# Another order of the instructions of the first two heads in a fused attention and soft mixture-of-experts kernel

## The chip, the cores and the metric

The kernel runs on one core of one Trainium2 chip. Times are device microseconds (us) of one execution. A timed run gives one time for the whole program; a profiled execution also gives a trace, whose span runs from the first to the last recorded instruction.

The engines have short names in the rows: PE is TensorE (matrix products), PEld its weight loads, DVE is VectorE, ACT is ScalarE, POOL is GpSimd, and SP the engine that issues nearly all DMA transfers. Each engine takes its own instructions in the order in which they stand in the program, and waits on semaphores for the others.

## The reference

Attention over 8 x 12 heads with 448 rows of 64, causal, and behind it a soft mixture of 8 experts over the 3584 rows of the result:

```
scores = scale * q @ k.T, masked above the diagonal
attn   = exp(scores - max(scores, -1)), divided by its row sum
x      = attn @ v, heads side by side: 3584 x 768
logits = x @ phi                               # 3584 x 32 slots
d      = softmax of logits over the rows       # slot_input = d.T @ x
slot_out[e] = relu(slot_input[e] @ w1[e]) @ w2[e]
out    = softmax of logits over the slots @ slot_out
```

## The kernel before

**Heads and pairs.** The 96 heads are handled one after another by a loop over `i`. Two heads make a pair `p`, whose queries and keys are loaded together; each arrives on 128 partitions as two copies of its 64 rows. In what follows "head 2" is the third head, the first of pair 1.

**What one head needs.** Products are done in a rounded type, with a second product that brings back what rounding lost:

1. `cast_k`, `cast_q` (ACT) round the keys and queries into `ks` and `qd`. `sub_k`, `sub_q` (POOL, or DVE where it says so) subtract the rounded from the raw values: the difference of the keys goes into the lower half of `ks`, that of the queries into `r2` (shown as `r` in rows). `copy_k2` (ACT) copies the rounded keys into `k2` (shown as `k`).
2. `scores1` (PE) multiplies `ks` by `qd` into a PSUM tile `s`, after small products with `tri` that set the causal mask. There are three such tiles, so head i+3 waits until head i has left its tile.
3. `max_evac` (ACT) copies one block row of `s` into `mx`, and `max_keys` 0 to 4 (DVE) take the maximum over the other blocks, transpose in blocks of 32 and reduce, into `r`. `max_row` 0 (PE) transposes that into `rt`, `max_row` 1 (DVE) reduces it into `mr`, and `max_spread` (POOL, an affine select) spreads the negated maximum over 14 rows of `r2`.
4. `scores2` (PE) multiplies `k2` by `r2` onto the same `s`: it adds the correction of the queries and subtracts the maximum. It can't start before `max_spread` of its head.
5. `exps` (ACT) takes the exponential into `pt`, `attv` (PE) multiplies by the values into `po`, and `norm` (DVE) divides.

**The loop.** A table `ORDER` gives the order of these steps in an iteration, one row for the first and one for the second head of a pair. Iteration `i` does the first products of head i+2, the second products and exponential of head i, and `attv` and `norm` of head i-1. So heads 0 and 1, and the first part of head 2, are done before the loop, in an order written out by hand, and the first two iterations leave out steps of the table.

**Warming products.** `warm(n)` issues n products of 128x512 columns that nobody reads; `START` has their numbers at three places of the start.

**Other work of POOL.** The list `later` holds small jobs (memsets and selects for the second half of the kernel); one is taken at the end of an iteration from `i` = 1 on, so they stand between the spreads and differences of the first heads.

**Loads.** SP issues the loads of keys, queries and values in one queue. Those of pair 0 come in halves (one head each), so that work can start early; pair 1's keys and queries are whole loads. The weights of the experts fill 22 resident buffers during attention, and the rest is loaded when buffers of attention come free near its end.

Of the kernel before, what the change touches and what calls it, by code (L numbers as in the profile page):

```python
# [33 lines left out]
RES, TW1 = 22, 12  # L34
WN, PAD = 1536, 24
WARM = (3, 2, 4, 2)
START = (6, 7, 4)

# [40 lines left out]
def attention_soft_moe(ctx: ExitStack, tc: tile.TileContext, qk, va, phi, w1, w2, out):  # L81
    nc = _Core(tc)
# [95 lines left out]
    def warm(n, w=None):  # L178

        w = misc("warm") if w is None else w  # L180
        for _ in range(n):
            nc.tensor.matmul(w, identb, tri.unsqueeze(1).to_broadcast([P, 4, P]),
                             start=True, stop=True)


    def cast_q(p, hs=slice(0, 2)):
        if p < NPAIR:
            nc.scalar.activation(out=qd_[p % NR][:, hs], in_=st["raw", 0, p][:, hs], func=AF.Copy)

    def cast_k(p, hs=slice(0, 2)):  # L190
        if p < NPAIR:
            nc.scalar.activation(out=ks_[p % NR][:, hs], in_=st["raw", 1, p][:, hs], func=AF.Copy)

    def sub_k(p, hs=slice(0, 2), eng=None):
        if p < NPAIR:
            ks = ks_[p % NR][64:P, hs]
            (eng or nc.gpsimd).tensor_tensor(out=ks, in0=st["raw", 1, p][64:P, hs], in1=ks, op=ALU.subtract)

    def copy_k2(p, hs=slice(0, 2)):
        if p < NPAIR:  # L200
            nc.scalar.activation(out=k2_[p % NR][64:P, hs], in_=ks_[p % NR][0:64, hs],
                                 func=AF.Copy)

    def sub_q(p, hs=slice(0, 2), eng=None):
        if p < NPAIR:
            (eng or nc.gpsimd).tensor_tensor(out=r2_[p % NR][64:P, hs], in0=st["raw", 0, p][64:P, hs],
                                             in1=qd_[p % NR][64:P, hs], op=ALU.subtract)
# [29 lines left out]
    def scores1_all(i):  # L237
        for part in ("c0", "k3", "c3", "c12", "k2", "k1", "k0"):
            scores1(i, part)

    def max_evac(i):
        if i < NHD:
            st["mx", i] = (xtp.tile([P, S], F32, tag="xt", name="mx1", bufs=2) if i == 1
                           else mx_)
            nc.scalar.activation(out=st["mx", i], in_=st["s", i][:, SC0:SC0 + S], func=AF.Copy)

    def max_keys(i, k):
        if i >= NHD:
            return
        if k < 3:  # L250
            s, mx = st["s", i], st["mx", i]
            c, w = k + 1, S - CQ0[k + 1]
            nc.vector.tensor_tensor(out=mx[:, CQ0[c]:S], in0=s[:, SCOL[c]:SCOL[c] + w],
                                    in1=mx[:, CQ0[c]:S], op=ALU.max)
        elif k == 3:
            nc.vector.transpose(out=mt_, in_=st.pop(("mx", i)))
        else:
            r = st["r", i] = wk.tile([P, NQB], F32, tag="r", name=f"r{i}", bufs=2)
            nc.vector.tensor_reduce(out=r, in_=mt_.rearrange("p (b k)->p b k", k=32),
                                    axis=AX.X, op=ALU.max)  # L260

    def max_row(i, k):
        if i >= NHD:
            return
        if k == 0:
            st["rt", i] = misc(f"rt{i}")
            nc.tensor.transpose(out=st["rt", i][0:NQB, 0:P], in_=st.pop(("r", i)), identity=ident)
        else:
            mr = st["mr", i] = wk.tile([NQB, 32], F32, tag="mr", name=f"mr{i}", bufs=2)
            nc.vector.tensor_reduce(out=mr, in_=st.pop(("rt", i))[0:NQB, 0:P].rearrange("p (g t)->p t g", g=4),  # L270
                                    axis=AX.X, op=ALU.max, negate=True)

    def max_spread(i):
        if i >= NHD:
            return
        p, h = divmod(i, 2)
        mr = st.pop(("mr", i))

        nc.gpsimd.affine_select(out=r2_[p % NR][0:NQB, h].rearrange("p (b t)->p b t", t=32),
                                in_=mr.unsqueeze(1).to_broadcast([NQB, NQB, 32]),  # L280
                                compare_op=ALU.is_equal, fill=0.0, base=0,
                                pattern=[[-1, NQB], [0, 32]], channel_multiplier=1)

    def scores2(i, cs):
        if i >= NHD:
            return
        p, h = divmod(i, 2)
        s = st["s", i]
        k2, r2 = k2_[p % NR], r2_[p % NR]
        for c in cs:  # L290
            w, m = S - CQ0[c], min(P, S - P * c)
            nc.tensor.matmul(s[0:m, SCOL[c]:SCOL[c] + w], k2[:, h, P * c:P * c + m],
                             r2[:, h, CQ0[c]:S], start=False, stop=True, skip_group_check=True)

    def exps(i):
        if i < NHD:
            nc.scalar.activation(out=pt_[i % 2][:, 0:1024], in_=st.pop(("s", i)), func=AF.Exp, scale=SCALE)
# [149 lines left out]
            plan[o + 19] = lambda b=b: dispatch(b, 1)  # L447


    warm(START[0])  # L450
    h0, h1 = slice(0, 1), slice(1, 2)
    for hs in (h0, h1):
        cast_k(0, hs)
        cast_q(0, hs)
        sub_k(0, hs, nc.vector)
        sub_q(0, hs)
    scores1_all(0)
    scores1_all(1)
    warm(START[1])
    max_evac(0)  # L460
    copy_k2(0, h0)
    max_evac(1)
    cast_k(1, h0)
    cast_k(1, h1)
    cast_q(1, h0)
    copy_k2(0, h1)
    cast_q(1, h1)
    for i, k in ((0, 0), (0, 1), (0, 2), (0, 3), (1, 0), (0, 4), (1, 1), (1, 2)):
        max_keys(i, k)
    sub_k(1, h0)  # L470
    max_row(0, 0)
    scores1_all(2)
    warm(START[2])
    max_evac(2)
    max_row(0, 1)
    max_spread(0)
    max_keys(1, 3)
    max_keys(1, 4)
    sub_k(1, h1, nc.vector)
    sub_q(1, h0)  # L480


    sid = const.tile([P, NSLOT], F32, name="sid")
# [24 lines left out]
    for i in range(NHD + 1):  # L508
        p, h = divmod(i, 2)
        if h:  # L510
            load_qk(p + 3, 1)
            if p + 1 < NPAIR - 1:
                loads_v(p + 1)
            load_qk(p + 3, 0)
            if p % 2 and nload < RES:
                load_w(nload)
                nload += 1
        if i == NHD - 3:

            loads_v(NPAIR - 1, nc.scalar)  # L520
        if i < 2:
            scores2(i, (1, 0, 2))
            if i:
                scores1_all(3)
                max_evac(3)
            scores2(i, (3,))
            exps(i)
            if i == 0:
                max_row(1, 0)
                max_row(1, 1)  # L530
                max_spread(1)
                sub_q(1, h1)

        qs = [int(n[1]) for n in ORDER[h] if n[0] == "a"]
        first = qs[:2] if qs[0] == 3 else qs[:1]
        for n in ORDER[h]:
            if i < 2 and (n in ("ev", "exp") or n[0] in "kt" or n in ("c0", "c3", "c12")):
                continue
            if i == 0 and n in ("mr0", "mr1", "sp"):
                continue  # L540
            if n[0] == "k" or n in ("c0", "c3", "c12"):
                scores1(i + 2, n)
            elif n[0] == "t":
                scores2(i, (int(n[1]),))
            elif n[0] == "a":
                attv(i - 1, (int(n[1]),), first)
            elif n[0] == "x":
                max_keys(i + 2, int(n[1]))
            elif n[0] == "n":
                norm(i - 1, int(n[1]))  # L550
            elif n in ("mr0", "mr1"):
                max_row(i + 1, int(n[2]))
            elif n == "ld":
                if i % 12 == 5 and i > 12:
                    logits_d(i // 12 - 1, lt)
            elif n == "pre":
                pre.get(i, int)()
            elif n == "plan":
                if later and i:
                    later.pop(0)()  # L560
                plan.get(i, int)()
            else:
                {"ev": lambda: max_evac(i + 2), "exp": lambda: exps(i), "sp": lambda: max_spread(i + 1),
                 "ck": lambda: cast_k(p + 2), "sk": lambda: sub_k(p + 2), "cq": lambda: cast_q(p + 2),
                 "c2": lambda: copy_k2(p + 1), "sq": lambda: sub_q(p + 2)}[n]()
        if i == NHD - 1:

            ps = [ps_s.tile([P, 1024], F32, tag="s", name=f"e{k}") for k in range(3)]
            logits_a(NB - 1, (2, 3, 4), ps[0], first=True, last=True)
            logits_t(NB - 1, 1)  # L570

            ph5 = xtp.tile([P, S], F32, tag="xt", name="ph5", bufs=2)[:, 0:P]
            nc.gpsimd.tensor_copy(out=ph5, in_=phis[1][:, 2].unsqueeze(1).to_broadcast([P, 4, NSLOT]))
# [238 lines left out]
```

## Time and profile before

| | us |
|---|---|
| median of 3 runs | 467.39 |
| lowest and highest of these | 465.57, 467.95 |
| the profiled execution's own time | 466.73 |
| its span | 465.0 |

The profiled execution lies between the lowest run and the median; 1.7 us of its time lie outside the span. PE is busy for 93% of the span, DVE for 77%, ACT for 72% and POOL for 59%. These are averages over the attention loop, the change of stages near 375 us, and a last stage in which weights stream in. A change at the start has to be read from the rows of the first 50 us.

### The profile page before, as it was taken

How to read it: one execution, taken by the hardware profiler on the slowest of the kernel's cores; microseconds unless marked ns; L12 is line 12 of the kernel's file. 1: busy time of each engine (PE TensorE's matmuls, PEld its weight loads, DVE VectorE, ACT ScalarE, POOL GpSimd, SP SyncE). 2: the span in 40 equal slices, each digit the busy share in tenths (PEclk: the TensorE clock that was granted, in tenths of full speed). 3: DMA queues.
4: the chain of work that ended last, by engine and by line, in shares of the span. 5: the costliest groups of instructions: out<-in, count | busy, mean ns of one | idle time of the engine just before them, and what ended most of it. 6: DMA issues, size and time to landing. Idle time of an engine off the chain costs nothing.

```text
span 465.0 us, 11809 instructions
## 1 busy us (share of the span) xinstructions
PE 432.1 (93%) x4458; PEld 363.3 (78%) x4458; DVE 356.9 (77%) x1056; ACT 334.2 (72%) x492; POOL 272.4 (59%) x226
## 2 busy tenths in 40 slices
PE   7899999999999999999999999999999999998650
PEld 3798999899899989998999899989989564543220
DVE  5898889888988898899889988988897267523350
ACT  6888898899888979897889789889985211422240
POOL 5898787778777877787777777777873000000000
PEclk9999999999999999999999999999999999999995
DMA  7387767676567666776666776677748989999998
GB/s 257 117 270 232 225 175 234 229 233 215 173 227 245 227 197 189 219 258 211 194 210 214 238 232 187 212 224 233 222 135 307 339 344 418 422 424 421 404 399 327
DMA packets 38200, 119.02 MB, mean 256 GB/s; under 512 B 4096, under 2 KB 11776, under 8 KB 38144
## 3 DMA queue, kind: packets, MB, share of 16 engines
q1 hardware_dynamic: 38000, 118.01, 73.9%
q8 instruction: 35, 0.57, 0.5%
q10 hardware_dynamic: 144, 0.27, 0.2%
q14 instruction: 21, 0.17, 0.1%
HBM read 107.25 MB, written 11.01 MB: 254 GB/s over the span
## 4 chain that ended last, share of the span: by engine, by line
PE 76%; DMA 12%; DVE 2%; ACT 2%; POOL 1%; issue 1%; POOLq 0%; ACTq 0%; SPq 0%
PE po L65 35%; PE s L65 25%; DMA w<-in_w_dram 12%; PE xt L65 5%; PE g L65 2%; PE sp L65 2%; PE rt L65 2%; PE pp L65 1%; PE tp L65 1%; PE hp L65 1%; POOL r L65 1%; PE e L65 1%; ACT ot L65 1%; PE lp L65 1%; POOL ks L65 0%
## 5 line engine op out<-in xcount | busy, mean ns | idle before, releaser
L65 PE MATMUL po<-va,pt 128*128 128x65 f32 (+1 forms) x1920 | 195.9, 250 | 0.1
L65 PEld LDWEIGHTS po<-va,pt 128*128 128x128 f32 (+1 forms) x1920 | 192.6, 171 | 1.3 <-issue 1.0
L65 DVE TENSOR_TENSOR mx<-s,mx 128x320 f32<-128x320 f32 (+2 forms) x288 | 100.6, 349 | 24.6 <-ACT mx L65 21.1
L65 ACT ACTIVATE pt<-s 128x1024 f32<-128x1024 f32 x96 | 98.1, 1021 | 10.9 <-PE s L65 6.7
L65 POOL TENSOR_TENSOR r<-qk,qd 64x896 fp32r<-64x896 f32 (+1 forms) x50 | 101.4, 2029 | 6.8 <-ACT qd L65 2.9
L65 POOL TENSOR_SCALAR_AFFINE_SELECT r<-mr 14x448 fp32r<-14x448 f32 x96 | 61.4, 640 | 73.5 <-DVE mr L65 72.9
L65 POOL TENSOR_TENSOR ks<-qk,ks 64x896 fp32r<-64x896 f32 (+1 forms) x47 | 98.0, 2086 | 5.1 <-ACT ks L65 1.5
L65 PE MATMUL s<-r,k 128*128 128x320 f32 (+3 forms) x384 | 85.0, 300 | 2.6 <-POOL r L65 2.5
L65 PE MATMUL s<-qd,ks 128*128 128x448 f32 (+3 forms) x384 | 77.0, 311 | 1.3 <-DVE ks L65 1.2
L65 ACT ACTIVATE mx<-s 128x448 f32<-128x448 f32 x96 | 52.3, 545 | 30.6 <-PE s L65 29.2
L65 PEld LDWEIGHTS s<-r,k 128*128 128x128 f32 (+1 forms) x384 | 60.0, 176 | 9.1 <-issue 3.7
L65 DVE STREAM_TRANSPOSE mt<-mx 128x448 f32<-128x448 f32 x96 | 61.9, 645 | 3.3
L65 DVE TENSOR_REDUCE r<-mt 128x14 f32<-128x448 f32 x96 | 58.5, 609 | 0.1
L65 PEld LDWEIGHTS s<-qd,ks 128*128 128x128 f32 (+1 forms) x384 | 55.8, 183 | 2.8 <-ACT qd L65 2.0
L65 ACT ACTIVATE ks<-qk 128x896 fp32r<-128x896 f32 (+1 forms) x50 | 45.5, 912 | 3.0 <-DMA qk<-in_qk_dram 3.0
L65 ACT ACTIVATE k<-ks 64x896 fp32r<-64x896 f32 (+1 forms) x49 | 45.8, 934 | 1.2
L65 ACT ACTIVATE qd<-qk 128x896 fp32r<-128x896 f32 (+1 forms) x50 | 46.0, 920 | 0.2
L65 PEld LDWEIGHTS <-identb 128*128 128x128 bf16 x316 | 28.0, 102 | 21.9 <-issue 18.0
L65 DVE TENSOR_TENSOR x<-po,sm 128x256 f32<-128x256 f32 x96 | 40.7, 424 | 3.3
L65 PE MATMUL s<-tri,identb 128*128 128x64 bf16 (+2 forms) x288 | 40.3, 236 | 0.1
L65 ACT ACTIVATE xts<-xt 128x448 f32<-128x448 f32 x47 | 25.4, 541 | 8.2 <-PE xt L65 6.4
L65 PE MATMUL so<-w,ht 128*32 128x384 f32 x256 | 24.7, 492 | 5.9 <-DMA w<-in_w_dram 4.1
(121 smaller groups left out, 417.9 us busy)
## 6 DMA issues: line engine op xcount, KB each, us to landing
w<-in_w_dram SPq DMA_DIRECT2D x64, 768.0 KB, 7.2
qk<-in_qk_dram SPq DMA_DIRECT2D x94, 448.0 KB, 3.4
va<-in_va_dram SPq DMA_DIRECT2D x47, 260.0 KB, 3.5
out_dram<-ot SPq DMA_DIRECT2D x28, 384.0 KB, 7.8
qk<-in_qk_dram SPq DMA_DIRECT2D x4, 224.0 KB, 3.6
va<-in_va_dram ACTq DMA_DIRECT2D x1, 260.0 KB, 3.4
phi<-in_phi_dram SPq DMA_DIRECT2D x2, 48.0 KB, 4.4
```

What stands on the lines that cost most here:

```text
L65: return self._tc.keep_in_program_order(op(*args, **kwargs))
```

## The change

The order of the start is written anew, and two differences of the keys go from DVE to POOL.

- Before the loop, the casts and differences of both heads of pair 0 came first, then the first products of heads 0 and 1, then seven warming products. Now the first head's keys are copied and its scores evacuated before the second head's keys and queries are cast, and four warming products stand between the first products of the two heads. Four further warming products behind the first products of head 2 are gone: 10 in all instead of 17.
- `sub_k` of head 1 and of head 3 run on POOL; before, DVE did them.
- `scores2` and `exps` of head 0 stand ahead of the loop; `sub_q` of heads 1, 2 and 3 come later in POOL's order.
- The first iteration of the loop is written out: `cast_k` and `sub_k` of pair 2, the first products of head 3, part of `attv` of head 0, then `scores2` and `exps` of head 1. The second iteration leaves out what was done there. From iteration 2 on nothing is different.

The core of the diff:

```diff
-START = (6, 7, 4)
+START = (6, 4)
...
-    for hs in (h0, h1):
-        cast_k(0, hs)
-        cast_q(0, hs)
-        sub_k(0, hs, nc.vector)
-        sub_q(0, hs)
+    cast_k(0, h0)
+    cast_q(0, h0)
+    sub_k(0, h0, nc.vector)
+    sub_q(0, h0)
+    copy_k2(0, h0)
     scores1_all(0)
+    max_evac(0)
+    cast_k(0, h1)
+    cast_q(0, h1)
+    sub_k(0, h1)
+    for k in range(5):
+        max_keys(0, k)
+    warm(START[1])
     scores1_all(1)
-    warm(START[1])
-    max_evac(0)
-    copy_k2(0, h0)
+    cast_k(1, h0)
+    copy_k2(0, h1)
+    sub_k(1, h0)
     max_evac(1)
...
+    cast_q(1, h0)
+    for k in range(3):
+        max_keys(1, k)
+    scores1_all(2)
+    cast_k(1, h1)
+    max_evac(2)
+    sub_k(1, h1)
+    scores2(0, (1, 0, 2, 3))
+    sub_q(0, h1)
     max_keys(1, 3)
     max_keys(1, 4)
-    sub_k(1, h1, nc.vector)
-    sub_q(1, h0)
+    exps(0)
+    cast_q(1, h1)
+    max_row(1, 0)
+    max_row(1, 1)
+    max_spread(1)
...
+        if i == 0:
+            for k in range(3):
+                max_keys(2, k)
+            cast_k(2)
+            scores1_all(3)
+            max_evac(3)
+            attv(0, (0, 3), (0,))
+            sub_k(2)
+            max_keys(2, 3)
+            max_keys(2, 4)
+            scores2(1, (1, 0, 2, 3))
+            sub_q(1, h0)
+            copy_k2(1)
+            exps(1)
+            attv(0, (2, 1), ())
+            cast_q(2)
+            continue
...
+            elif n == "sq" and i == 1:
+                sub_q(1, h1)
+                sub_q(2)
```

On POOL the start now reads as follows, up to the spread of head 3. A row has the line, the operation, what it writes and reads, and the shape; `qk_0`, `qk_1`, `qk_2` are the raw keys or queries of pairs 0, 1 and 2, a row that writes `ks` is a `sub_k`, one that writes `r` from `qk` a `sub_q`, and an AFFINE_SELECT is a `max_spread`. Where two rows read alike, the first is the pair's first head, the second its second. Before:

```order
L65 TENSOR_TENSOR r_123<-qk_0_95,qd_118 64x448 x2
L65 TENSOR_TENSOR ks_121<-qk_1_99,ks_121 64x448
L65 AFFINE_SELECT r_123<-mr_210 14x448
L65 TENSOR_TENSOR r_125<-qk_1_101,qd_120 64x448
L65 AFFINE_SELECT r_123<-mr_237 14x448
L65 TENSOR_TENSOR r_125<-qk_1_101,qd_120 64x448
L65 TENSOR_TENSOR ks_119<-qk_2_104,ks_119 64x896
L65 AFFINE_SELECT r_125<-mr_278 14x448
L65 TENSOR_TENSOR r_123<-qk_2_106,qd_118 64x896
L65 MEMSET run_m_226 128x1
L65 AFFINE_SELECT r_125<-mr_324 14x448
```

And of the change, from the second difference on (the first, `sub_q` of head 0, is the same):

```order
L65 TENSOR_TENSOR ks_119<-qk_0_93,ks_119 64x448
L65 TENSOR_TENSOR ks_121<-qk_1_99,ks_121 64x448
L65 AFFINE_SELECT r_123<-mr_186 14x448
L65 TENSOR_TENSOR ks_121<-qk_1_99,ks_121 64x448
L65 TENSOR_TENSOR r_123<-qk_0_95,qd_118 64x448
L65 AFFINE_SELECT r_123<-mr_216 14x448
L65 TENSOR_TENSOR ks_119<-qk_2_104,ks_119 64x896
L65 TENSOR_TENSOR r_125<-qk_1_101,qd_120 64x448
L65 AFFINE_SELECT r_125<-mr_275 14x448
L65 TENSOR_TENSOR r_125<-qk_1_101,qd_120 64x448
L65 TENSOR_TENSOR r_123<-qk_2_106,qd_118 64x896
L65 MEMSET run_m_227 128x1
```

Two differences of 64x448 have come in (the `ks` rows of head 1 and head 3), and of the two `sub_q` of pair 1 both now stand behind the spread of head 1; before, one stood ahead of it.

On ACT, from the first cast to the cast of pair 2's keys; a row `mx` is a `max_evac`, `k` a `copy_k2`, `pt` an `exps`. Before:

```order
L65 ACTIVATE ks_119<-qk_0_93 128x448
L65 ACTIVATE qd_118<-qk_0_95 128x448
L65 ACTIVATE mx<-s_151 128x448
L65 ACTIVATE k_122<-ks_119 64x448
L65 ACTIVATE mx_177<-s_159 128x448
L65 ACTIVATE ks_121<-qk_1_99 128x448 x2
L65 ACTIVATE qd_120<-qk_1_101 128x448
L65 ACTIVATE k_122<-ks_119 64x448
L65 ACTIVATE qd_120<-qk_1_101 128x448
L65 ACTIVATE mx<-s_196 128x448
L65 ACTIVATE pt_85<-s_151 128x1024
L65 ACTIVATE ks_119<-qk_2_104 128x896
```

And of the change, from the two casts of head 1 on:

```order
L65 ACTIVATE ks_119<-qk_0_93 128x448
L65 ACTIVATE qd_118<-qk_0_95 128x448
L65 ACTIVATE ks_121<-qk_1_99 128x448
L65 ACTIVATE k_122<-ks_119 64x448
L65 ACTIVATE mx_182<-s_171 128x448
L65 ACTIVATE qd_120<-qk_1_101 128x448
L65 ACTIVATE ks_121<-qk_1_99 128x448
L65 ACTIVATE mx<-s_193 128x448
L65 ACTIVATE pt_85<-s_148 128x1024
L65 ACTIVATE qd_120<-qk_1_101 128x448
L65 ACTIVATE ks_119<-qk_2_104 128x896
```

The cast of pair 1's first keys now stands ahead of head 1's evacuation, and the second cast of pair 1's queries stands between `exps` of head 0 and the cast of pair 2's keys.

## Rows read from the trace of the kernel before

**Rows 1.** Window: length, busy us (instructions) of five engines, clock, DMA share, GB/s.

```profile
15.20:40.70 25.50, 23.89 (x235) 22.26 (x235) 23.22 (x69) 22.30 (x29) 23.82 (x26) 1.00 0.57 178
```

**Rows 2.** Timeline of POOL, 4 to 46.5 us: start, us, operation [idle before <-releaser].

```profile
10.16 1.13 POOL L65 TENSOR_TENSOR ks<-qk,ks 64x448 fp32r<-64x448 f32 x1 [1.51 <-ACT ks L65]
...
15.21 0.64 POOL L65 TENSOR_SCALAR_AFFINE_SELECT r<-mr 14x448 fp32r<-14x448 f32 x1 [0.87 <-DVE mr L65]
15.93 1.15 POOL L65 TENSOR_TENSOR r<-qk,qd 64x448 fp32r<-64x448 f32 x1
17.03 2.08 POOL L65 TENSOR_TENSOR ks<-qk,ks 64x896 fp32r<-64x896 f32 x1
19.19 0.64 POOL L65 TENSOR_SCALAR_AFFINE_SELECT r<-mr 14x448 fp32r<-14x448 f32 x1
19.91 2.10 POOL L65 TENSOR_TENSOR r<-qk,qd 64x896 fp32r<-64x896 f32 x1
...
22.24 0.64 POOL L65 TENSOR_SCALAR_AFFINE_SELECT r<-mr 14x448 fp32r<-14x448 f32 x1
...
40.07 0.64 POOL L65 TENSOR_SCALAR_AFFINE_SELECT r<-mr 14x448 fp32r<-14x448 f32 x1
...
46.28 0.64 POOL L65 TENSOR_SCALAR_AFFINE_SELECT r<-mr 14x448 fp32r<-14x448 f32 x1 [0.49 <-DVE mr L65]
```

**Rows 3.** Timeline of PE, 1 to 14.5 us and 40 to 42 us.

```profile
7.84 1.20 PE L65 MATMUL s<-qd,ks 128*128 128x192 f32 x3
8.85 2.85 PE L65 MATMUL warm<-tri,identb 128*128 128x512 bf16 x7
...
12.03 0.71 PE L65 MATMUL s<-qd,ks 128*128 128x192 f32 x3
12.58 1.04 PE L65 MATMUL warm<-tri,identb 128*128 128x512 bf16 x4
13.27 0.82 PE L65 MATMUL s<-r,k 128*128 128x320 f32 x4
...
40.77 0.73 PE L65 MATMUL s<-r,k 128*128 128x448 f32 x3 [0.79 <-POOL r L65]
```

**Rows 4.** The tail: timeline of SP, 340 to 400 us.

```profile
346.84 52.97 SPq L65 DMA_DIRECT2D w<-in_w_dram  x30
```

**Rows 5.** Timeline of ACT, 3 to 23 us.

```profile
9.08 0.54 ACT L65 ACTIVATE mx<-s 128x448 f32<-128x448 f32 x1 [0.60 <-PE s L65]
9.52 1.03 ACT L65 ACTIVATE ks<-qk 128x448 fp32r<-128x448 f32 x2
10.55 0.58 ACT L65 ACTIVATE qd<-qk 128x448 fp32r<-128x448 f32 x1
11.15 0.57 ACT L65 ACTIVATE k<-ks 64x448 fp32r<-64x448 f32 x1
...
12.83 0.55 ACT L65 ACTIVATE mx<-s 128x448 f32<-128x448 f32 x1 [0.51 <-ACT qd L65]
14.13 1.02 ACT L65 ACTIVATE pt<-s 128x1024 f32<-128x1024 f32 x1 [0.75 <-PE s L65]
15.05 0.94 ACT L65 ACTIVATE ks<-qk 128x896 fp32r<-128x896 f32 x1
```

**Rows 6.** DMA issued from 2.5 to 3 us: size, us from issue to landing.

```profile
qk<-in_qk_dram SPq DMA_DIRECT2D x1, 448.0 KB, 6.8
```

**Rows 7.** Timeline of DVE, 3.8 to 17.8 us.

```profile
6.84 0.62 DVE L65 TENSOR_TENSOR ks<-qk,ks 64x448 fp32r<-64x448 f32 x1 [2.17 <-ACT ks L65]
...
13.58 1.25 DVE L65 TENSOR_TENSOR ks<-qk,ks 64x448 fp32r<-64x448 f32 x1
14.86 0.28 DVE L65 TENSOR_REDUCE mr<-rt 14x32 f32<-14x128 f32 x1
15.17 1.14 DVE L65 TENSOR_TENSOR mx<-s,mx 128x192 f32<-128x192 f32 x3
...
17.02 0.62 DVE L65 TENSOR_REDUCE r<-mt 128x14 f32<-128x448 f32 x1
```

More of the change, by code (lines that the diff above doesn't have):

```diff
@@ L451, in attention_soft_moe @@
     h0, h1 = slice(0, 1), slice(1, 2)
-    for hs in (h0, h1):
-        cast_k(0, hs)
-        cast_q(0, hs)
-        sub_k(0, hs, nc.vector)
-        sub_q(0, hs)
-    scores1_all(0)
+    cast_k(0, h0)
[3 more added lines that the diff above has]
+    copy_k2(0, h0)
+    scores1_all(0)
+    max_evac(0)
[5 more added lines that the diff above has]
+    warm(START[1])
     scores1_all(1)
-    warm(START[1])
-    max_evac(0)
-    copy_k2(0, h0)
+    cast_k(1, h0)
+    copy_k2(0, h1)
+    sub_k(1, h0)
     max_evac(1)
[L463 to L470, printed above, removed]
     max_row(0, 0)
-    scores1_all(2)
-    warm(START[2])
-    max_evac(2)
     max_row(0, 1)
     max_spread(0)
+    cast_q(1, h0)
[7 more added lines that the diff above has]
+    sub_q(0, h1)
     max_keys(1, 3)
     max_keys(1, 4)
-    sub_k(1, h1, nc.vector)
-    sub_q(1, h0)
+    exps(0)
[3 more added lines that the diff above has]
+    max_spread(1)
     sid = const.tile([P, NSLOT], F32, name="sid")
@@ L520, in attention_soft_moe @@
             loads_v(NPAIR - 1, nc.scalar)
[L521 to L532, printed above, removed]
+        if i == 0:
[15 more added lines that the diff above has]
+            continue
         qs = [int(n[1]) for n in ORDER[h] if n[0] == "a"]
@@ L536, in attention_soft_moe @@
         for n in ORDER[h]:
-            if i < 2 and (n in ("ev", "exp") or n[0] in "kt" or n in ("c0", "c3", "c12")):
-                continue
-            if i == 0 and n in ("mr0", "mr1", "sp"):
+            if i == 1 and (n in ("ev", "exp", "c0", "c3", "c12", "c2") or n[0] in "kta"):
                 continue
```

## The prediction, written before the changed kernel ran

> **What bounds the kernel now.** PE is busy for 93% of the span and POOL for 59%, which says little about a change that touches only the first 20 us. I read the timelines of that start engine by engine, POOL first, because the change gives it work. Its idle times end with the spread (affine select) of head 1 at 15.21, which waited 0.87 us for the row maximum from DVE; the next idle time shown is at 46.28, ahead of the spread of head 10 [rows 2]. Between 15.20 and 40.70, which is 25.50 us, POOL is busy for 23.82 us in 26 instructions, so some 0.07 us lie between two of them; the five columns are PE, PEld, DVE, ACT and POOL [rows 1]. That is POOL working without a pause on differences, spreads and the small jobs of the `later` list. PE feels it: at 40.77 the second products of head 8 have waited 0.79 us for POOL's spread, which began at 40.07 [rows 2, 3]. At 46.28 it is POOL that waits, for DVE's maximum, which follows PE's first products [rows 2]. So the start has two parts: up to 15 us a net of short waits between all engines, and from there to 41 us a queue of POOL work of fixed length; after that PE sets the pace and the time carries over. The tail doesn't take a shift back: 30 loads of weights are issued over 52.97 us from 346.84 on [rows 4], in the buffers that attention leaves, so an attention that ends later starts them later.
>
> The question is therefore when POOL gets through its list up to head 3's spread, the first place behind which before and change have the same POOL order. Before, that spread began at 22.24 [rows 2].
>
> **The change, part by part.** First ACT, since POOL's differences wait for casts. The cast of pair 1's first keys needs a whole load, which lands 6.8 us after an issue between 2.5 and 3 us [rows 6], so not much before 9.5; before, that cast began at 9.52 [rows 5]. In the new order it stands in front of head 1's evacuation, which ran at 9.08 before [rows 5]. ACT can't pass it, so everything behind it starts from 9.52 at the earliest. I add start-to-start steps [rows 5]: cast to cast 1.03/2; 0.60 from a cast to a small copy (10.55 to 11.15), which I also take from a small copy to the next operation and from a cast to a cast with another wait; an evacuation gives way after 0.44 (9.08 to 9.52).
>
> - Cast of head 2's keys 9.52; `copy_k2` of head 1 10.05; evacuation of head 1 10.65; cast of head 2's queries 11.09, done at 11.67; cast of head 3's keys 11.69, done at 12.27.
> - PE then does the first products of head 2, its three large ones from about 11.85. Before, the evacuation began 0.80 after those three (12.03 to 12.83) and the next products in the queue 0.55 after them (12.03 to 12.58) [rows 3, 5]. So the evacuation of head 2 falls at 12.65, and the second products of head 0 at 12.40, where they stood at 13.27: the four warming products at 12.58 are gone. The exponential followed the second products by 0.86 (13.27 to 14.13): now 13.26.
> - Behind the exponential, after 0.92 (14.13 to 15.05), now stands the cast of head 3's queries: 14.18. The cast of pair 2's keys comes 0.60 later, at 14.78, and takes 0.94: done at 15.72. Before it began at 15.05 [rows 5].
>
> Now POOL. A difference of 64x448 takes 1.10 from start to start (15.93 to 17.03), one of 64x896 ahead of another operation 2.16 (17.03 to 19.19), a spread 0.72 (19.19 to 19.91), and `sub_q` of pair 2 with the memset behind it 2.33 (19.91 to 22.24) [rows 2].
>
> - `sub_k` of head 1 falls into the idle time that ended at 10.16 (1.51 us), and `sub_k` of head 2 starts at 10.16 as before [rows 2]. So the first of the two differences that leave DVE costs POOL nothing; with that gap filled it would cost 1.10.
> - The spread of head 0 follows at about 11.3: its row maximum no longer stands behind the seven warming products of 2.85 us at 8.85 [rows 3].
> - `sub_k` of head 3 waits for its cast, 12.32; `sub_q` of head 1 13.42; the spread of head 1 14.57, done at 15.21. Before, it began at 15.21. DVE has its maximum by then: the evacuation ends at 11.19, the steps from the first maximum to the end of the first reduction take 2.47 (15.17 to 17.64), and PE's transpose and the last reduction, at 0.28 each as an estimate from the latter's row, bring it to about 14.3 [rows 7]. DVE's own difference in front of it, 1.25 us at 13.58 where the same work took 0.62 at 6.84, is gone [rows 7].
> - `sub_k` of pair 2 waits for ACT until 15.77: 0.56 us of new idle time. Then 2.16 to `sub_q` of head 2 at 17.93, 1.10 to the spread of head 2 at 19.03, 0.72 to `sub_q` of head 3 at 19.75, 1.10 to `sub_q` of pair 2 at 20.85, 2.33 to head 3's spread at 23.18.
>
> Head 3's spread moves from 22.24 to 23.18: **0.94 us later**. Checked another way: head 1's spread is 0.64 earlier, behind it come 0.56 of idle time and, as one 64x448 `sub_q` more than before now stands there, 1.10; the rest, 0.08, is the pause behind the spread. From there POOL's list is the same and had no pause, so head 8's second products come at 41.7, and all that follows is later by the same amount: 466.73 + 0.94 = 467.7 for the profiled execution. The median of the three runs is 0.66 above that execution's time and the lowest 1.16 below it, so 467.7 is 0.3 above the median; I keep it as the forecast.
>
> Edits that I cost at nothing: the earlier evacuation and copy of head 0, since their consumer, the spread of head 0, waits for POOL until 11.3; with POOL free there it would come at most 1.13 earlier, the length of the `sub_k` in front of it, and head 1's spread, which waits for other casts, not at all. The products and `attv` of the first iteration lie between the spreads of heads 1 and 2, 14.6 and 19.0, where they had 15.2 to 19.2. ACT's cast of pair 2's queries, last of its row, ends near 19.2 (15.72 and one evacuation 0.54, a copy as long as a cast 0.94, an exponential 1.02, a cast 0.94), before POOL wants it at 20.85; each 0.1 beyond that would go into the sum. The load of pair 3's keys now waits for POOL's `sub_q` of head 1, done at 14.5; even with 6.8 to landing it is there at 21.3, and POOL's `sub_k` of pair 3 is due at 23.9.
>
> Bounds: if ACT isn't late, POOL has no idle time behind the spread of head 1, and the sum falls by 0.56 to +0.4. If PE runs at its lower clock when it reaches head 2, the three large products take 1.20 as at 7.84 instead of 0.71, and the second products, 0.82, some 0.57 more at the same ratio [rows 3]; the exponential and the casts behind it are then 1.06 later: +2.0. With these ends the forecast's own range is 467.1 to 468.7.
>
> **The clock.** Seven warming products took 2.85 us at 8.85, four of the same shape 1.04 at 12.58 [rows 3]: 0.41 each against 0.26. So PE ran at its lower level (1.2 GHz) to the end of the seven and at the higher (2.4 GHz) behind them, after having work without a break from 7.84 on. In the new order PE has products from the start to the end of the four warming products behind head 0, which should bring the rise sooner, but little to do from about 10 to 11.8. The Trainium skill, TensorE: Matmul & The Clock Gate, Part 1, says that the array starts throttled, that sustained activity releases it and that a stretch without work throttles it again. The trace agrees on the rise; by the fall, which no row of this start shows, the second rival would come true.
>
> **Rivals.**
>
> - *PE and ACT decide, not POOL's list.* If the spreads are held by the maxima from DVE rather than by POOL's own work, what counts is that the second products of head 0 come at 12.40 instead of 13.27: -0.87, so 465.9. For it speaks that PE has only 0.79 us of waiting at 40.77 [rows 3], so the two chains lie close. Against it: no spread from 19.19 to 40.07 shows an idle time ahead of it [rows 2]. If the two effects cancel, the time is 466.7.
> - *Slower: the clock.* If PE is at the lower level from 11.8 until the loop has run for some microseconds, the first and second products of heads 2, 0, 3 and 1 take 0.5 to 0.6 more each, together some 2.2 us, and the first full iteration of the loop, 3.6 us per head by the spreads of heads 3 and 8 (22.24 and 40.07) [rows 2], up to twice as long. Less PE's 0.8 of waiting that is +4 to +5: 471 to 472. It decides if PE's little work between 10 and 11.8 brings a fall. For it: 10 warming products instead of 17. Against it: the three products behind the wait at 40.77 ran at 0.73, so a wait of 0.79 left the clock up [rows 3].
>
> **How the numbers follow.** POOL's list sets the time, 467.1 to 468.7: 0.62. PE and ACT decide or the two cancel, 464.8 to 466.9: 0.22. The clock, 469 to 472: 0.16. The runs before spread over 2.4 us, so 0.5% of 467.39, 2.3 us, is about what a measurement can tell from no change: below 465.05 and above 469.73. Faster by more takes the low end of the second case and its run-to-run spread, 0.10; slower takes most of the third and the upper end of the first, 0.16; within is the rest, 0.74. The range leaves out the ends of the two rivals: 465.4 to 470.0.
>
> **What would show it.** In the changed kernel's profile: ACT's cast of head 2's keys near 9.52 with an idle time ahead of it, and head 1's evacuation near 10.6; `sub_k` of pair 2 on POOL near 15.8 after an idle time put down to ACT; head 3's spread near 23.2; no idle time on POOL from there to about 46; PE's wait for POOL near 41.7. It is wrong if POOL shows idle times put down to DVE's maximum between 16 and 40, if head 3's spread is before 22.2, or if the large products of head 2 take 1.2 us.

## The result, and the profile after

| us | before | after |
|---|---|---|
| median of 11 runs | 467.18 | 469.26 |
| lowest, highest | 465.22, 468.21 | 467.61, 469.98 |
| the profiled execution's own time | 466.73 | 467.9 |
| its span | 465.0 | 466.2 |

The change is slower by 2.1 us: the ratio is 1.0047, with an interval of 1.0029 to 1.0064, just inside the 0.5% that the prediction counts as no change, and clear of 1. The profiled execution of after is the second fastest of its 11 runs; the step from before's profiled execution to it is only 1.17 us. The other runs lost more, and their granted clock, a mean over the whole execution, is mostly lower (0.967 to 0.976 in seven runs, at 468.8 to 470.0 us; 0.980 to 0.984 in four, at 467.6 to 469.3). What that mean can tell is taken up below.

The timeline of POOL after, from 10 us on (start, us, operation, idle before), answers to [rows 2]:

```profile
10.35 0.64 POOL L65 TENSOR_SCALAR_AFFINE_SELECT r<-mr 14x448 fp32r<-14x448 f32 x1 [0.43 <-DVE mr L65]
...
13.47 0.64 POOL L65 TENSOR_SCALAR_AFFINE_SELECT r<-mr 14x448 fp32r<-14x448 f32 x1
14.51 2.08 POOL L65 TENSOR_TENSOR ks<-qk,ks 64x896 fp32r<-64x896 f32 x1 [0.40 <-ACT ks L65]
...
19.02 0.64 POOL L65 TENSOR_SCALAR_AFFINE_SELECT r<-mr 14x448 fp32r<-14x448 f32 x1 [1.33 <-DVE mr L65]
...
23.17 0.64 POOL L65 TENSOR_SCALAR_AFFINE_SELECT r<-mr 14x448 fp32r<-14x448 f32 x1
...
40.96 0.64 POOL L65 TENSOR_SCALAR_AFFINE_SELECT r<-mr 14x448 fp32r<-14x448 f32 x1
```

The four spreads of heads 0 to 3 are at 10.35, 13.47, 19.02 and 23.17, head 8's at 40.96. Head 3's and head 8's are 0.93 and 0.89 later than in [rows 2], and no idle time is shown between them: that is the forecast, to a few hundredths. But POOL did not get there on the forecast path. Head 1's spread is 1.1 us earlier than forecast, and at 19.02 there is an idle time of 1.33 us for DVE's maximum, which the prediction named as a sign against it.

The cause of that wait is two engines away. PE's timeline after, against [rows 3]:

```profile
8.85 0.71 PE L65 MATMUL s<-qd,ks 128*128 128x192 f32 x3
...
10.75 0.21 PE L65 MATMUL s<-qd,ks 128*64 128x64 f32 x1 [0.80 <-ACT qd L65]
...
10.88 0.71 PE L65 MATMUL s<-qd,ks 128*128 128x192 f32 x3
...
13.88 1.20 PE L65 MATMUL s<-qd,ks 128*128 128x192 f32 x3
...
16.04 1.20 PE L65 MATMUL s<-r,k 128*128 128x320 f32 x4
...
18.28 0.27 PE L65 MATMUL rt<-ident,r 128*14 128x128 f32 x1
...
41.65 0.73 PE L65 MATMUL s<-r,k 128*128 128x448 f32 x3 [0.81 <-POOL r L65]
```

The large products of heads 1 and 2 take 0.71, those of head 3 take 1.20. The windows of the same stretch (length, busy us of PE, PEld, DVE, ACT and POOL, granted clock, DMA share, GB/s):

```profile
8.00:9.00 1.00, 0.30 (x4) 0.30 (x5) 0.93 (x3) 0.85 (x2) 0.86 (x2) 1.00 1.06 417
9.00:10.00 1.00, 0.89 (x6) 0.37 (x5) 0.55 (x2) 0.71 (x2) 0.92 (x1) 1.00 1.01 247
10.00:11.00 1.00, 0.25 (x4) 0.28 (x5) 0.97 (x3) 1.00 (x3) 0.64 (x1) 1.00 0.71 247
11.00:12.00 1.00, 1.00 (x9) 0.88 (x7) 0.93 (x3) 0.45 (x2) 0.84 (x1) 1.00 0.80 267
12.00:13.00 1.00, 0.26 (x3) 0.13 (x2) 0.62 (x1) 1.00 (x2) 1.00 (x2) 1.00 0.06 21
13.00:14.00 1.00, 0.55 (x6) 0.30 (x4) 0.86 (x3) 1.00 (x3) 0.93 (x2) 0.91 0.67 104
14.00:17.00 3.00, 3.00 (x19) 2.91 (x18) 1.61 (x5) 1.92 (x3) 2.60 (x3) 0.50 0.93 355
17.00:18.00 1.00, 1.00 (x11) 1.00 (x9) 0.80 (x3) 0.72 (x1) 0.69 (x1) 0.88 0.04 14
```

The granted clock is full to 13, as the products of 0.71 bear out, falls late in the microsecond from 13 to 14, is half (1.2 GHz) from 14 to 17, and returns in the next one. Ahead of the fall PE worked in pieces, with waits for ACT and for DVE between them: 2.70 of the five microseconds from 8 to 13. At the lower clock PE is busy without a pause, so the transpose of head 2's maximum (18.28), which stands behind all of it in PE's queue, is late, and so is DVE's reduction, which here waits 0.83 us for it:

```profile
18.66 0.28 DVE L65 TENSOR_REDUCE mr<-rt 14x32 f32<-14x128 f32 x1 [0.83 <-PE rt L65]
```

Last, ACT's timeline and the DMA issue of pair 1's first keys (its last column is us to landing), against [rows 5, 6]:

```profile
8.13 0.58 ACT L65 ACTIVATE ks<-qk 128x448 fp32r<-128x448 f32 x1 [0.23 <-DMA qk<-in_qk_dram]
...
9.60 0.54 ACT L65 ACTIVATE mx<-s 128x448 f32<-128x448 f32 x1 [0.29 <-PE s L65]
```

```profile
qk<-in_qk_dram SPq DMA_DIRECT2D x1, 448.0 KB, 5.4
```

The keys landed 5.4 us after their issue, not 6.8, so the cast in front of head 1's evacuation began at 8.13 instead of the forecast 9.52. The early landing and the lower clock all but cancel at head 3's spread: that it stands at 23.17, where 23.18 was forecast, is luck.

### The profile page after: what moved, and what is told of

It is laid out like the page before. It is cut to its first block, busy times and chain, and to the rows that moved or that the text cites. A ratio compares the mean times of both kernels' runs of the same rounds, so it can differ in the third digit from the quotient of the medians.

```text
span 466.2 us, 11793 instructions
## 1 busy us (share of the span) xinstructions
PE 432.8 (93%) x4451; PEld 364.5 (78%) x4451; DVE 355.6 (76%) x1054; ACT 334.3 (72%) x492; POOL 274.6 (59%) x228
## 4 chain that ended last, share of the span: by engine, by line
PE 75%; DMA 13%; POOL 4%; ACT 2%; issue 1%; DVE 1%; SPq 0%; POOLq 0%; DVEq 0%; ACTq 0%
PE po L65 33%; PE s L65 24%; DMA w<-in_w_dram 10%; PE xt L65 5%; PE g L65 2%; PE sp L65 2%; POOL r L65 2%; PE hp L65 2%; PE rt L65 2%; POOL ks L65 2%; DMA out_dram<-ot 2%; PE pp L65 1%; DMA qk<-in_qk_dram 1%; PE tp L65 1%; PE e L65 1%
## 5 line engine op out<-in xcount | busy, mean ns | idle before, releaser
L65 POOL TENSOR_TENSOR ks<-qk,ks 64x896 fp32r<-64x896 f32 (+1 forms) x49 | 100.3, 2047 | 5.8 <-ACT ks L65 2.1
L65 PEld LDWEIGHTS <-identb 128*128 128x128 bf16 x309 | 27.0, 101 | 20.3 <-issue 16.7
```

Of the source, the lines that this page charges most:

```text
L65: return self._tc.keep_in_program_order(op(*args, **kwargs))
```

## The experiments

All of them compute the whole reference; the added warming products are read by nobody. Each ratio is against the kernel before on the same chip. It need not equal the ratio of the two medians. Each kernel has one profiled execution, and what is read from its timeline holds for that one.

**1. Warming products put back where PE waits.** This tells the clock from POOL's list: it adds work to PE and takes none from POOL.

```diff
     for k in range(3):
         max_keys(1, k)
+    warm(2)
     scores1_all(2)
...
     scores2(0, (1, 0, 2, 3))
+    warm(3)
     sub_q(0, h1)
...
             cast_k(2)
+            warm(2)
             scores1_all(3)
```

> The changed kernel with seven warming products put where PE waits: two ahead of the first products of head 2, three behind the second products of head 0, two ahead of the first products of head 3. Theory 1 (the clock: PE's little work from 8 to 13.8 lets the clock fall, so that the products of heads 3, 0 and 1 run at 1.2 GHz and head 2's spread waits 1.33 for its maximum): the three large products of head 3 take 0.71 instead of 1.20, head 2's spread on POOL starts near 17.8, head 3's near 22.0, and the time falls by 1.5 to 2.5, to 467 (a ratio to before of 0.998 to 1.001). Rival (POOL's longer list costs the 0.9): head 3's spread stays near 23.2 and the time at 469.

Measured: 466.62 (465.9 to 469.59, 12 runs), ratio 1.000 [0.998, 1.0021]. The loss of 2.1 us is gone. Its timelines, PE first and then the spreads of heads 1, 2, 3 and 8 on POOL:

```profile
13.88 0.71 PE L65 MATMUL s<-qd,ks 128*128 128x192 f32 x3
```

```profile
13.33 0.64 POOL L65 TENSOR_SCALAR_AFFINE_SELECT r<-mr 14x448 fp32r<-14x448 f32 x1
...
17.61 0.64 POOL L65 TENSOR_SCALAR_AFFINE_SELECT r<-mr 14x448 fp32r<-14x448 f32 x1
...
21.77 0.64 POOL L65 TENSOR_SCALAR_AFFINE_SELECT r<-mr 14x448 fp32r<-14x448 f32 x1
...
39.57 0.64 POOL L65 TENSOR_SCALAR_AFFINE_SELECT r<-mr 14x448 fp32r<-14x448 f32 x1
```

Head 3's products begin at 13.88 as in after, but take 0.71; the wait of 1.33 ahead of head 2's spread is gone. Against after, the spreads are 0.14, 1.41, 1.40 and 1.39 earlier and the profiled execution's time is 1.55 shorter: 1.27 us come in between heads 1 and 2, where the clock is the difference, and stay through attention. PE was busy for 3.86 of the five microseconds from 8 to 13, instead of 2.70. The runs fall into two groups, eight from 465.9 to 467.2 and four from 468.5 to 469.6; the four have clocks of 0.974 to 0.980, the eight 0.981 to 0.984.

**2 and 3. The differences of heads 1 and 3 back on DVE**, in after (2) and in kernel 1 (3):

```diff
-    sub_k(0, h1)
+    sub_k(0, h1, nc.vector)
...
-    sub_k(1, h1)
+    sub_k(1, h1, nc.vector)
```

> The changed kernel with the differences of the keys of heads 1 and 3 back on DVE. Rival (POOL's longer list costs the 0.9): POOL has two 64x448 differences less, so head 3's spread comes 1.0 earlier, near 22.2, and the time falls by about 1, to 468.2. Theory 1 (clock): head 2's spread still waits for its maximum behind slow products, so the time stays at 469, within 0.4.

> Both edits of the two kernels before: seven warming products where PE waits and the two differences back on DVE. If only the clock costs: 467, as with the warming products alone. If only POOL's list costs: 468.2. If each costs a part and the shorter list can be used once the maximum comes early: head 3's spread near 21 and 466.0 to 466.5.

Measured: 470.52 (469.6 to 471.08, 6 runs), ratio 1.0065 [1.0048, 1.0083], and 470.36 (469.17 to 470.78, 6 runs), ratio 1.006 [1.0042, 1.0079]. Both miss: giving POOL less work made it slower, by 1.3 us against after and by 3.7 against kernel 1. DVE and POOL of kernel 2 show why:

```profile
12.28 1.40 DVE L65 TENSOR_TENSOR ks<-qk,ks 64x448 fp32r<-64x448 f32 x1
```

```profile
12.05 1.14 POOL L65 TENSOR_TENSOR r<-qk,qd 64x448 fp32r<-64x448 f32 x1
15.92 0.64 POOL L65 TENSOR_SCALAR_AFFINE_SELECT r<-mr 14x448 fp32r<-14x448 f32 x1 [2.72 <-DVE mr L65]
```

In this order head 3's difference stands on DVE in front of the transpose of head 1's maximum. It takes 1.40 beside a difference on POOL, against 0.62 alone [rows 7], and head 1's spread falls from 13.47 to 15.92 with 2.72 us of idle time. Head 1's difference costs too: on DVE it stands in front of head 0's maximum, and head 0's spread comes at 11.33 in kernel 2 and 11.36 in kernel 3, against 10.35 in after and 10.20 in kernel 1. Kernel 3 has the same, 1.41 us for that difference and head 1's spread at 15.84, while its clock is full until about 16.6 (0.81 in the window from 16 to 17); so it is the place on DVE that costs, not the clock alone. The keys landed later in these two (6.1 and 6.5 us), but the evacuation of head 1 that waits for them is over by 10.96 in kernel 3, and DVE takes up head 1's maximum only at 11.15, behind head 0's. In kernel 2 the clock falls too, already near 10.9 (0.94 in the window from 10 to 11, 0.50 in the next), and stays down longer than in after; its windows:

```profile
12.00:14.00 2.00, 1.44 (x6) 1.16 (x5) 1.91 (x3) 1.07 (x2) 1.14 (x1) 0.50 0.06 18
14.00:22.00 8.00, 6.84 (x39) 6.66 (x40) 4.72 (x13) 5.16 (x7) 3.97 (x4) 0.50 0.44 148
22.00:26.00 4.00, 4.00 (x30) 3.59 (x29) 3.41 (x10) 2.49 (x4) 3.79 (x5) 0.68 0.01 4
```

**4. The opposite: those two differences on POOL, in the kernel before.**

```diff
-        sub_k(0, hs, nc.vector)
+        sub_k(0, hs, nc.vector if hs is h0 else None)
...
-    sub_k(1, h1, nc.vector)
+    sub_k(1, h1)
```

> The kernel before with only one part of the change: the differences of the keys of heads 1 and 3 on POOL. If POOL's list costs what it adds: the second difference pushes head 1's spread from 15.21 to about 15.5 and the first delays the products of head 1 by 0.5, together 0.3 to 0.9, so 467.5 to 468.1. If the clock is all: no change, 467.2.

Measured: 467.74 (466.09 to 470.23, 12 runs), ratio 1.001 [0.9992, 1.0028]: not clear of before, though the median lies in the range of the first theory. In the trace the spreads of heads 1 and 3 stay at 15.21 and 22.25. So 2.2 us of added POOL work cost little where DVE's maxima left POOL waiting anyway. It may have cost some 0.3: in this trace the loads landed earlier (pair 1's keys after 5.0 us) and head 0's spread came at 12.19 instead of 12.48, a lead that is gone at head 1's, where POOL no longer shows an idle time. With kernels 2 and 3, this part of the change isn't its loss.

**5. Fewer warming products alone, in the kernel before.**

```diff
-START = (6, 7, 4)
+START = (6, 4, 0)
```

> The kernel before with the change's number of warming products and nothing else of it: 6 and 4 instead of 6, 7 and 4. Clock: PE has less work ahead of the first products of head 2, the rise comes later or is lost, and the time rises by 1 to 2.5, to 468.3 to 469.8. Rival (the order alone made the change slower, the number of warming products doesn't matter): within 0.4 of before, or 0.5 faster, because the row maximum of head 0 no longer stands behind seven of them.

Measured: 467.66 (466.26 to 470.63, 12 runs; before 466.76 in 33), ratio 1.0036 [1.0015, 1.0057]. The median is 0.9 longer than before's, less than the 1 to 2.5 expected, and the ratio gives 1.7. Head 1's spread comes 1.26 earlier than before, 13.95: in front of head 0's transpose stand four products, which take 1.04 at the full clock, where seven at the lower one took 2.85 [rows 3]. Then the clock falls; windows, PE and POOL of this kernel:

```profile
13.00:14.00 1.00, 0.00 (x0) 0.00 (x0) 0.94 (x3) 1.00 (x2) 0.13 (x2) 1.00 0.79 307
14.00:17.00 3.00, 2.36 (x13) 2.06 (x14) 2.24 (x5) 1.53 (x3) 2.92 (x3) 0.68 0.71 223
```

```profile
8.04 1.04 PE L65 MATMUL warm<-tri,identb 128*128 128x512 bf16 x4
...
15.57 1.20 PE L65 MATMUL s<-qd,ks 128*128 128x192 f32 x3
```

```profile
18.86 0.64 POOL L65 TENSOR_SCALAR_AFFINE_SELECT r<-mr 14x448 fp32r<-14x448 f32 x1 [1.02 <-DVE mr L65]
```

Head 3's large products take 1.20 and head 2's spread waits 1.02 for its maximum: the picture of after, in the old order. By then 0.93 of the 1.26 us are lost (19.19 in [rows 2]), and at head 8's spread, 40.06, nothing is left of them. So in this trace the fall of the clock eats a gain and no more: the last head's spread begins at 358.53, before's at 358.50, and the 0.6 us by which the span is longer lie behind attention. That fewer products make the old order slower is shown by the runs; that the clock at the start is why is not.

**6. Still more warming products**: kernel 1 with `START` (6, 6), three instead of two ahead of head 2's first products, and three at the start of iteration 2.

> The changed kernel with the seven warming products that brought it to 466.6 and six more: two more behind head 0's first products, one more ahead of head 2's, three at the start of iteration 2, where PE waits for a cast. Four of twelve executions with seven were at 468.5 to 469.6, the others at 465.9 to 467.2. If those four are executions in which the clock still fell, more products make them rare: median 466.3 and at most one run in six above 468. If their cause is another, the two groups stay, and the median too.

Measured: 467.7 (466.82 to 468.69, 10 runs), ratio 1.0027 [1.0011, 1.0042], where 466.3 was expected, though every run's mean clock was 0.981 to 0.987, and in the trace the clock does not fall before 450. Not the clock at the start, then. ACT of this kernel:

```profile
9.30 0.58 ACT L65 ACTIVATE ks<-qk 128x448 fp32r<-128x448 f32 x1 [0.78 <-DMA qk<-in_qk_dram]
...
10.50 0.54 ACT L65 ACTIVATE mx<-s 128x448 f32<-128x448 f32 x1
```

Here the keys took 6.6 us to land. The cast stands idle for 0.78, and head 1's evacuation follows at 10.50: the forecast's 9.52 and 10.65, shifted by 0.2. Head 3's spread is at 22.82, head 8's at 40.61. Whether the later landing belongs to the added products or to that execution is not settled.

**7 and 8. The kernel before, and kernel 6, with two memsets of the list moved ahead**, behind `sub_q` of head 0 where POOL is idle:

```diff
+    nc.gpsimd.memset(si, 0.0)
+    nc.gpsimd.memset(lt, 0.0)
...
-             lambda: nc.gpsimd.memset(si, 0.0), lambda: nc.gpsimd.memset(lt, 0.0), lambda: nc.gpsimd.memset(gs, 0.0),
+             lambda: None, lambda: None, lambda: nc.gpsimd.memset(gs, 0.0),
```

> The kernel before with two of POOL's small jobs, the memsets of 0.74 and 0.52 us that stood between the spreads of heads 4 to 6, moved into POOL's idle time behind its first difference. If POOL's list sets the time from 15 to 41 us: head 8's spread comes 0.8 to 1.3 earlier, and the time falls by 0.8 to 1.0 (to 466.4), less than 1.3 because PE has only 0.8 of waiting there. If the maxima from DVE hold the spreads (PE and ACT decide): no change.

> The changed kernel with thirteen warming products more and the two memsets of POOL moved into its idle time at 6 to 7.3 us. If both the clock and POOL's list count: 465.3 to 465.7, faster than before by 0.3 to 0.4%. If the list doesn't count: as without the memsets moved, 466.3.

Measured in the kernel before: 465.83 (465.12 to 468.09, 12 runs), ratio 0.9986 [0.9968, 1.0004]. The list is shorter by 1.26 us; POOL of this kernel at the spreads of heads 5, 6 and 8:

```profile
28.84 0.64 POOL L65 TENSOR_SCALAR_AFFINE_SELECT r<-mr 14x448 fp32r<-14x448 f32 x1 [0.65 <-DVE mr L65]
...
32.12 0.64 POOL L65 TENSOR_SCALAR_AFFINE_SELECT r<-mr 14x448 fp32r<-14x448 f32 x1 [0.45 <-DVE mr L65]
...
39.67 0.64 POOL L65 TENSOR_SCALAR_AFFINE_SELECT r<-mr 14x448 fp32r<-14x448 f32 x1
```

Head 8's spread gains 0.40 of the 1.26; the rest turns into waits for DVE's maxima. So POOL's list does set the time in the kernel before, but by some 0.4 us only. In kernel 6 the same edit gave 466.47 (465.86 to 468.79, 12 runs), ratio 1.0007 [0.9993, 1.0021], 1.2 less than without it; its profiled execution had the keys after 4.8 us, so the landing may have a part in that. Head 8's spread is at 38.96 there, 1.11 earlier than before, but that did not reach the end: the span, 465.3, is 0.3 longer than before's.

**9 and 10. The landing made late**, in kernel 1 (9) and in the kernel before (10): pair 1's keys are loaded behind its queries and pair 0's values.

```diff
-    load_qk(1, 1)
     load_qk(1, 0)
     loads_v(0)
+    load_qk(1, 1)
```

> The changed kernel with the seven warming products, and pair 1's keys loaded behind its queries and the values of pair 0, so that they land some 1 to 2 us later than the 8.0 us of the profiled execution with the products alone. If the cast that waits for them gates the start (it stands in front of head 1's evacuation): the evacuation of head 1, head 1's spread and head 3's spread all move by what the landing moves beyond 8.0, and the time rises by 1 to 2, to 467.6 to 468.6. If POOL's idle time and the waits for PE hide it: within 0.4 of 466.6.

> The kernel before with the same change of the loads' order. There the cast of pair 1's keys stands behind head 1's evacuation, so a landing near 10.5 delays only the first products of head 2 and POOL's differences: 0.3 to 1.0 slower, 467.2 to 467.8. If the place of the cast makes no difference, the loss is as large as in the changed kernel.

Measured: 470.08 (468.27 to 470.77, 12 runs), ratio 1.0052 [1.0031, 1.0073], for the new order; 467.6 (466.25 to 469.03, 12 runs), ratio 0.9992 [0.9969, 1.0015], for the old one, 0.6 above the median of before's 29 runs but not clear of it. ACT of both, the new order first:

```profile
10.44 0.58 ACT L65 ACTIVATE ks<-qk 128x448 fp32r<-128x448 f32 x1 [2.64 <-DMA qk<-in_qk_dram]
...
11.64 0.54 ACT L65 ACTIVATE mx<-s 128x448 f32<-128x448 f32 x1
```

```profile
8.87 0.54 ACT L65 ACTIVATE mx<-s 128x448 f32<-128x448 f32 x1
10.31 1.04 ACT L65 ACTIVATE ks<-qk 128x448 fp32r<-128x448 f32 x2 [0.89 <-DMA qk<-in_qk_dram]
```

The keys are cast at nearly the same time, 10.44 and 10.31. In the old order head 1's evacuation has passed ahead of them, at 8.87, and head 3's spread comes at 21.93, no later than in [rows 2]. In the new order it waits behind the cast until 11.64, and PE waits with it; PE of kernel 9:

```profile
12.79 0.28 PE L65 MATMUL s<-qd,ks 128*64 128x64 f32 x1 [2.61 <-ACT qd L65]
...
13.02 1.20 PE L65 MATMUL s<-qd,ks 128*128 128x192 f32 x3
```

During this wait of 2.61 us the clock falls in spite of the warming products (0.71 in the window from 11 to 12), and it is down until past 18. Kernel 9 loses 3.5 us to kernel 1, where 1 to 2 were expected: in this trace, which is that of its slowest run, the late landing takes the clock with it.

**11. Kernel 1 with the two memsets moved ahead.**

> The changed kernel with the seven warming products and the two memsets moved into POOL's idle time at 6 to 7.3 us. If the list counts on top of the clock: 465.4 to 465.9, the fastest of all, 0.2 to 0.3% below before; head 8's spread near 39.0. If the maxima hold the spreads by then: 466.3.

Measured: 466.21 (465.49 to 467.04, 12 runs), ratio 0.9982 [0.9961, 1.0002]. It is the best of the new order and 3.0 us below after, but it isn't clear of the kernel before, and neither is the old order with the same edit. In its trace head 8's spread is at 38.91, as expected, 1.16 earlier than before; the median is only 0.8 below before's.

## Why the prediction came out as it did

The forecast, 467.7, is 1.6 us below the median of after, 469.26, which lies inside the range; the sign of the shift was right. The reason given for it was half of the story: POOL's list, at 0.62, was to give 467.1 to 468.7, and the median lies in what the clock, at 0.16, was to give, 469 to 472.

- **POOL's list, and carrying over.** Right in after: from head 3's spread to 46 us no idle time, head 8's spread +0.89, the wait of PE for it at 41.65 (forecast 41.7), the span +1.2. The last spreads of attention, in before, after and kernel 8:

```profile
358.50 0.64 POOL L65 TENSOR_SCALAR_AFFINE_SELECT r<-mr 14x448 fp32r<-14x448 f32 x1 [3.02 <-DVE mr L65]
```

```profile
359.41 0.64 POOL L65 TENSOR_SCALAR_AFFINE_SELECT r<-mr 14x448 fp32r<-14x448 f32 x1 [3.02 <-DVE mr L65]
```

```profile
357.44 0.64 POOL L65 TENSOR_SCALAR_AFFINE_SELECT r<-mr 14x448 fp32r<-14x448 f32 x1 [3.02 <-DVE mr L65]
```

  The shift of 0.9 carries over to 359.41; the remaining 0.3 us come behind it, and what takes them isn't settled. From the last spread to the end of the span the traces take 106.5 us (before) to 107.9 (kernel 8), so up to 1.4 us of one execution's time can come from behind attention, more than many of the effects weighed here. Kernel 7 adds that the list is ahead of DVE's maxima by only 0.4 us, so the rival in which PE and ACT decide was nearer than its chance.
- **The chain through ACT and POOL to head 3's spread.** Right in the traces at the full clock, once the landing is put in. The sum had the cast at 9.52 and the spread at 23.18. With the cast at 8.00, as in kernel 1, the same steps give 21.66, measured 21.77; with 9.30, as in kernel 6, they give 22.96, measured 22.82. The copy of head 1 at 10.05 is a slip of 0.07: with the step of 0.60 that the sum itself names it is 10.12.
- **"Lands 6.8 us after an issue ... so not much before 9.5".** This step failed as a number. In [rows 5] no wait for a load stands ahead of the cast at 9.52; it followed an evacuation, so the row showed only that the keys were there by then. Over the profiled executions the same load took from 4.8 us (kernel 8) through 5.3 (1), 5.4 (after) and 6.6 (6) to 6.8 (before). With after's 8.13 the sum gives 21.79, 0.45 earlier than before: no loss. The price of the cast's place is real, as kernels 9 and 10 show, but only where the keys land late.
- **The removed warming products, costed at nothing but what they freed.** This is the step that decided the time. They were treated as work in front of `scores2`; their absence was weighed only in the clock rival, at 0.16. In the profiled execution the lower clock costs 1.27 us at head 2's spread (kernel 1 against after). In the medians, kernel 1 against after, putting the products back is worth 2.6 us, all of the loss and some more (before took 467.29 us beside kernel 1 and 467.18 beside after); how much of that is the clock at the start, no trace shows beyond the 1.27. Kernel 5 has the loss in the old order as well, with the reservation made there. The bound of +2.0 for a lower clock at head 2 was above the 1.27, and at the wrong head: the fall came for head 3.
- **The clock rival's size.** +4 to +5 assumed that the clock stays down through the first full iteration. In the profiled execution it was down from about 13.8 to 17.2 (0.09 and 0.12 of a microsecond on either side of the three at 0.50, each divided by 0.5) and cost 1.27. In the other runs it may have lasted longer, but their lower mean clocks don't show that, since the mean is made mostly at the end of the execution, where PE has little or no work. Windows of before, then of after:

```profile
440.00:450.00 10.00, 7.36 (x28) 4.33 (x28) 7.56 (x15) 6.21 (x14) 0.00 (x0) 1.00 1.07 399
450.00:465.00 15.00, 0.00 (x0) 0.00 (x0) 0.00 (x0) 0.00 (x0) 0.00 (x0) 0.55 0.92 343
```

```profile
440.00:450.00 10.00, 8.17 (x29) 5.02 (x27) 6.65 (x13) 6.05 (x14) 0.00 (x0) 0.83 1.07 399
```

  By windows of 1 us, before is at the lower level for 13.5 us, all behind 450, and after for 18.9: 3.4 at the start, as much again from 443 to 447, and the rest at the end. The mean also misses what comes ahead of a trace's first record of the clock: before's windows read 1.00 from 7 to 9, where its products take 1.20 [rows 3]. Kernel 7's profiled execution has a mean of 0.975 and is 0.3 us faster than before's. So why after's median is 1.4 us above its profiled execution stays open; a later landing, which kernel 9 shows to be dear in this order, is as good a candidate as a longer stay at the lower clock.
- **The argument against that rival**, that a wait of 0.79 us at 40.77 left the clock up [rows 3], failed. The longest wait of PE between 8.85 and 13.88 in after is the one of 0.80 ahead of 10.75, just as long, and the clock fell. But the length of one wait does not decide it: before's own start has one of 1.70, and the products behind it ran at the full clock:

```profile
15.90 0.70 PE L65 MATMUL s<-r,k 128*128 128x320 f32 x3 [1.70 <-POOL r L65]
```

  What differs in these traces is what stood around the wait: several waits with short pieces of work between them in after, work without a pause from 7.84 to 14.20 ahead of it in before. No run tests that by itself. The Trainium skill, TensorE: Matmul & The Clock Gate, Part 1, ties the fall to a stretch without work, and under "A second HAM failure mode" also to a kernel in which PE is idle for short times between its groups of products often enough; this trace agrees with the second, with waits of 1.02, 0.80, 0.74 and 0.34 us ahead of the fall and short pieces of work between them.
- **The two differences moved to POOL.** The first cost POOL nothing, as forecast. What taking them from DVE is worth was undervalued: the prediction credited it with the 1.25 us of one difference, off the path. In the new order it is 3.7 us in the medians (kernel 3 against 1). At head 1's spread it is 2.5, since one of them would stand in front of head 0's maximum there (1.16) and the other in front of head 1's (1.41); behind that, kernel 3's clock falls.

Open: why the landing differs, and whether it goes by the kernel or by the execution; what the slower runs of after, and the four of kernel 1, have in common; and what takes the time behind attention.

## What to carry to other kernels

That nobody reads a filler product does not make it free to remove, on an engine whose granted clock can fall: when an order is tightened, look at what the engine does in the microseconds that the fillers leave, and put them where it waits. In an in-order queue, an instruction that waits for a load belongs behind work that is ready, because its landing can move: the same load took 4.8 to 6.8 us over these traces. One profiled execution can sit at the fast end of its kernel's runs, so a sum made against it should be checked against the spread of landings and of the clock at the place that matters. A mean clock of a whole execution doesn't tell where the clock was low.

## What was unexpected of the hardware

- PE fell to 1.2 GHz for some 3.4 us although it had been busy for 0.30, 0.89, 0.25, 1.00 and 0.26 of the five microseconds up to 13; with 0.45, 0.68, 0.89, 1.00 and 0.84 (kernel 1) it did not.
- The clock at the start differs between traces of the old order too, with all 17 warming products: the first large products, at about 5, take 1.20 in before and 0.71 in kernels 4 and 7, where the clock is then at 0.50 from about 8.2 to 11.6. Head 1's spread is at 15.21, 15.21 and 15.22 in the three, and at 14.88 in kernel 10, whose products from 8 on run at the full clock. By these four traces the lower clock costs little there, where most of PE's work is the seven products that nobody reads.
- A DVE difference of 64x448 with both inputs in SBUF takes 0.62 alone [rows 7] and 1.40 when it starts 0.23 behind a POOL difference of 1.14: it ends 0.49 us after POOL does. The Trainium skill, SBUF — State Buffer, section "Who interferes with whom", says that such an instruction gets its second input through a read interface shared with GpSimd, and contends with it; the rows agree, as do 1.41 in kernel 3 and 1.25 in before [rows 7], which also start beside a POOL difference.
